# Inverting the diagonal blocks of a chunked delta-rule recurrence 16 wide instead of 32 wide

## The chip, the cores and the metric

The kernel runs on one core of a Trainium2 chip. The core has five instruction streams that matter here: TensorE (PE for its products, PEld for the loading of their stationary operand), VectorE (DVE), ScalarE (ACT), GpSimd (POOL), and SyncE (SP), which issues the DMAs. Each runs its own instructions in the order in which they stand and waits for the others through semaphores. TensorE writes to PSUM only, and VectorE and ScalarE move results from there to SBUF. The metric is the device time of one execution in microseconds (us).

## The reference

An attention-like recurrence over 768 time steps (4 batches, 8 heads, head size 40) makes `y`, which then passes through a gated feed-forward block:

```python
for t in range(S):
    y[:, :, t] = np.einsum('bhd,bhde->bhe', rt, state)
    Sa = np.einsum('bhde,bhe->bhd', state, at)
    state_decay = state * wt[:, :, None, :] - np.einsum('bhd,bhe->bhde', Sa, bt)
    state = state_decay + np.einsum('bhd,bhe->bhde', vt, kt)
...
h = np.maximum(x @ w_in, 0.0)
u, v = (h[..., :d_ff // 2], h[..., d_ff // 2:])
v_n = (v - mu) / np.sqrt(var + 1e-06)
v_s = np.einsum('ts,bsd->btd', w_spatial, v_n) + b_spatial[None, :, None]
gated = u * v_s
return (gated @ w_out).astype(np.float32)
```

Everything is float32. What the state loses at a time step depends on the state that the step before left, so within a chunk of 64 time steps the corrections form a unit lower triangular system of 64 unknowns. Its inverse is what this change is about.

## The kernel before, in words

Phase 1 runs the recurrence and the first half of the feed-forward block, phase 2 the spatial product and the projection. Phase 1 has 24 steps (`NS`): 2 pairs of batches times 12 chunks of 64 times. A step handles 8 units (`NU`), each with two heads, one in the upper and one in the lower 64 partitions (`PR`).

For each step there is preparation and a chain. Preparation, some steps ahead: `prep_load` brings 774 KB of input in two DMAs, `scan1`, `scan2`, `at_mul` and `sl_mul` make `at` and `sl` on VectorE, `lprime` makes the two 32x32 diagonal blocks of each head's 64x64 matrix on TensorE, and `lblock` (L338) masks them on VectorE into `Lc`, which collects four steps (`GS`), a group. Six groups make the 24 steps.

`invert(g)` inverts the 32x32 blocks of a whole group on VectorE: a transpose (L346), thirty pairs of a product (L352, into PSUM as `itmp`) and an addition (L356), and two closing transposes (L361, L363) that give `XT0` and `X11`, the inverse and its transpose. Group 0 is inverted in one go ahead of step 0; the pieces of the later groups are spread over the steps before they are needed.

One step ahead of its use, the two 32x32 inverses of a head are joined into the inverse of its 64x64 matrix: `b_l21` (L459) makes the off-diagonal block, `b_zt` (L478) multiplies it with `XT0`, `b_x21` (L505) multiplies that with `X11`, and `b_xcopy` (three ACT copies, L770) puts the diagonal blocks into `xf`. Around them stand `b_lka` (L390), `b_tok` (L442, two transposes named tok0 and tok1 here) and `b_h` (L420), each with its copies on ACT.

The chain of a step: `c_bp` (L536) multiplies the state `Mc`, ACT copies (L546), `c_ff` (L554), a copy to `ffs` (L562), `c_xx` (L572) with `xf`, the xx copies (L583), POOL's triangular masks (`strict`, L397), `c_mp` (L606, L612), the new `Mc` on VectorE (L626, L630), `c_y` (L638) and its scaling on VectorE (L651). The next step's `c_bp` needs the new `Mc`, and needs L651 to have emptied its PSUM buffer.

The order is written out by hand: `at(t, fn, ...)` gives each piece a place in step time, the list is sorted by it, and each engine receives its instructions in that order. From step 11 on the products of the feed-forward block (L708, L753) are put in at four places of a step. PSUM has eight banks: two for `bk`, which all of `lprime`, `b_lka`, `b_tok`, `b_l21`, `b_zt`, `b_h` and `b_x21` share in turn, two for `ch`, two for `bp`, one each for `itmp` and `pv`. Whoever writes a third `bk` waits until the first has been emptied.

Of the kernel before, what the change touches and what calls it, by code (L numbers as in the profile page):

```python
# [25 lines left out]
GS = 4  # L26
WSEG = C + 2
# [184 lines left out]
def phase1(ctx, tc, early, late, vtok, win, xs, vns, uts, dscr):  # L212
# [14 lines left out]
    inv = pool("inv")  # L227
    xinv = pool("xinv")
# [24 lines left out]
    maskp = const.tile([P, C], F32, name="maskp")  # L253
    maskn = const.tile([P, C], F32, name="maskn")
# [78 lines left out]
    def lblock(s):  # L333
        if s % GS == 0:
            st["Lc", s // GS] = inv.tile([P, GS * NU, HB], F32, name="Lc")
        Lc = st["Lc", s // GS]
        u0 = (s % GS) * NU
        nc.vector.tensor_tensor(  # L338
            out=Lc[:, u0:u0 + NU, :], in0=st.pop(("pl", s)),
            in1=maskl.unsqueeze(1).broadcast_to([P, NU, HB]), op=ALU.mult,  # L340
        )
# [24 lines left out]
    INV_N = HB + 1  # L366
# [35 lines left out]
    def b_lka_out(s, par):  # L402
# [3 lines left out]
        if s in LKA_POOL:  # L406
            nc.scalar.activation(At[par][ev], pk[ev], AF.Copy)  # L407
# [63 lines left out]
    def b_zt(s):  # L471
        XT0, X11 = st["X", s // GS]
        u0 = (s % GS) * NU
        l21 = st["l21", s]
        m2 = ps_k.tile([P, NU, HB], F32, name="bk")
        for n in range(NU):
            for o in (0, 64):
                nc.tensor.matmul(  # L478
                    m2[o:o + HB, n, :], lhsT=l21[o + HB:o + 64, n, :],
                    rhs=XT0[o + HB:o + 64, u0 + n, :], start=True, stop=True,  # L480
# [96 lines left out]
    def c_xx_out(s, g):  # L577
# [3 lines left out]
        if s in TRI_POOL:  # L581
            for par in range(2):
                nc.scalar.activation(Rt[par][PR[par], gp], xx[PR[1 - par]], AF.Copy, scale=-1.0)  # L583
            for par in range(2):
                strict(Rt[par][PR[par], gp, 0:C], NP)
            return
        for par in range(2):
            nc.scalar.activation(Rt[par][PR[par], gp, C:], xx[PR[1 - par], :, C:], AF.Copy, scale=-1.0)
        for par in range(2):
            ur, ev = PR[par], PR[1 - par]  # L590
            nc.vector.tensor_tensor(
                out=Rt[par][ur, gp, 0:C], in0=xx[ev, :, 0:C],
                in1=maskn[ev].unsqueeze(1).broadcast_to([64, NP, C]), op=ALU.mult,
            )
# [178 lines left out]
    H_POOL, LKA_POOL, TRI_POOL = range(0, 99), range(0, 99), range(0, 99)  # L773
# [18 lines left out]
    for q in range(1, NS):  # L792
# [77 lines left out]
    with tc.manual_schedule():  # L870
# [20 lines left out]
        for m, val in ((maskp, 1.0), (maskn, -1.0)):  # L891
            p.memset(m, val)
            for rows in PR:
                p.affine_select(
                    out=m[rows], in_=m[rows], pattern=[[1, C]], base=0,
                    channel_multiplier=-1, compare_op=ALU.is_gt, fill=0.0,
                )
# [111 lines left out]
```

## Time and profile before

| | |
|---|---|
| three runs | 708.47, 710.8 and 714.62 us; median 710.8 |
| span of the profiled execution, first to last instruction | 709.5 us |
| TensorE products and loads | 11,136 each, products busy for 593.6 us (84%) |
| VectorE, ScalarE, GpSimd busy | 437.5, 414.7 and 290.3 us |
| first inversion on VectorE | 28.6 to 56.6 us |
| step ends (end of the second L651) | step 0: 71.3, 3: 145.9, 7: 227.9, 11: 307.1, 15: 388.6, 23: 545.3 us |
| granted TensorE clock, mean | 0.900 |

The execution's own time is not told apart from its span; the span lies among the three runs' times, 1.3 us under their median. A row of a timeline reads: start, length, engine, line, operation, output <- inputs, shape, how many were merged, and in brackets the idle time before it with what ended it. "issue" there is time in which the engine waited for nothing that the profile shows. In the table of busy time by stretch, the clock is the share of full speed that was granted.

### The profile page before, as it was taken

To read this page: it belongs to the slowest core of one execution; us is meant where nothing else is said; L and a number is where in the kernel's file an instruction comes from. 1 tells how busy PE (TensorE), PEld (TensorE's weight loads), DVE (VectorE), ACT (ScalarE), POOL (GpSimd) and SP (SyncE) were. 2 spreads that over 40 slices of the span, in tenths; PEclk is the share of its full clock that TensorE was granted. 3 is DMA by queue.
4 is the path that set the end of the run, shared out by engine and by line. 5 is a ranking of instruction groups with operands and counts; after the bars stand their busy time and mean duration, and the time that the engine had idled before them with its cause. 6 is when DMAs were issued, how large, how long until landed. Compare 5 with 4: busy or idle time off the path is not lost. (4 is left out here: it accounts for less than half of the span.)

```text
span 709.5 us, 26133 instructions
## 1 busy us (share of the span) xinstructions
PE 593.6 (84%) x11136; PEld 538.4 (76%) x11136; DVE 437.5 (62%) x862; ACT 414.7 (58%) x904; POOL 290.3 (41%) x486
## 2 busy tenths in 40 slices
PE   1707886587877789898997999999999999999997
PEld 1606785476766678787886788778888988999997
DVE  7897659977999899766688456612127521332221
ACT  2406754375565777587886889889855543331112
POOL 4102213212345444253464524545457982453221
PEclk9656978787797877899999899999999999999999
DMA  8443665273554724456536434344336454650001
GB/s 188 84 97 56 122 144 103 63 154 73 121 113 93 141 66 115 96 125 127 122 109 209 119 118 121 94 125 138 99 103 186 144 170 129 203 176 29 29 29 55
DMA packets 101339, 81.38 MB, mean 115 GB/s; under 512 B 33576, under 2 KB 90152, under 8 KB 99304
## 3 DMA queue, kind: packets, MB, share of 16 engines
q1 hardware_dynamic: 100680, 78.01, 44.0%
q10 hardware_dynamic: 544, 1.72, 1.1%
q8 instruction: 87, 1.43, 0.9%
q14 instruction: 28, 0.23, 0.1%
HBM read 59.20 MB, written 20.50 MB: 112 GB/s over the span
## 5 line engine op out<-in xcount | busy, mean ns | idle before, releaser
L397 POOL TENSOR_SCALAR_AFFINE_SELECT Rt<-Rt 64x512 f32<-64x512 f32 (+1 forms) x144 | 84.0, 585 | 99.4 <-ACT Rt L583 76.3
L546 ACT ACTIVATE Rt<-bp 64x416 f32<-64x416 f32 x96 | 49.1, 512 | 71.5 <-PE bp L536 69.5
L352 DVE TENSOR_TENSOR itmp<-A 128x30 f32<-128x30 f32 (+9 forms) x180 | 75.3, 419 | 3.2
L397 POOL TENSOR_SCALAR_AFFINE_SELECT At<-At 64x512 f32<-64x512 f32 x48 | 36.3, 756 | 96.5 <-ACT At L407 94.3
L536 PE MATMUL bp<-lin,Mc 40*64 40x104 f32 x768 | 53.5, 302 | 15.4 <-DVE y L651 11.7
L173 PE MATMUL pg<-wsh,vh 128*128 128x384 f32 x192 | 64.7, 337 | 0.0
L174 PE MATMUL pg<-wsl,vh 128*128 128x384 f32 x192 | 64.7, 337 | 0.0
L175 PE MATMUL pg<-wsh,vl 128*128 128x384 f32 x192 | 64.6, 336 | 0.0
L356 DVE TENSOR_TENSOR A<-A,itmp 128x30 f32<-128x30 f32 (+9 forms) x180 | 59.0, 328 | 6.2
L536 PEld LDWEIGHTS bp<-lin,Mc 40*64 40x64 f32 x768 | 46.7, 168 | 18.3 <-DVE y L651 13.7
L177 DVE TENSOR_TENSOR g<-pg,bb 128x384 f32<-128x384 f32 x32 | 17.8, 556 | 62.9 <-PE pg L175 59.1
L54 POOL TENSOR_TENSOR gl<-g,gh 128x384 fp32r<-128x384 f32 x32 | 33.9, 1064 | 50.2 <-ACT gh L50 50.0
L583 ACT ACTIVATE Rt<-ch 64x416 f32<-64x416 f32 x96 | 49.2, 512 | 4.5 <-PE ch L572 2.1
L554 PE MATMUL ch<-Rt,At 128*64 128x104 f32 x768 | 47.5, 283 | 0.0
L554 PEld LDWEIGHTS ch<-Rt,At 128*64 128x64 f32 x768 | 42.1, 158 | 4.5 <-issue 1.9
L50 ACT ACTIVATE gh<-g 128x384 fp32r<-128x384 f32 x32 | 16.6, 522 | 48.9 <-DVE g L178 48.8
L442 PE MATMUL bk<-ident,sl 128*128 128x128 f32 x192 | 31.1, 293 | 16.3 <-ACT tk L448 6.8
L572 PE MATMUL ch<-ffs,xf 64*64 64x104 f32 x768 | 43.4, 267 | 0.1
L54 POOL TENSOR_TENSOR vl<-raw,vh 128x512 fp32r<-128x512 f32 x24 | 32.3, 1353 | 26.2 <-ACT vh L50 13.9
L716 DVE BATCH_NORM_STATS2 bs<-vr 128x6 f32<-128x512 f32 x24 | 16.6, 691 | 41.6 <-ACT vr L710 41.5
L638 PE MATMUL bp<-Rt,tk 128*40 128x64 f32 x768 | 32.5, 240 | 10.1 <-issue 10.1
L572 PEld LDWEIGHTS ch<-ffs,xf 64*64 64x64 f32 x768 | 38.3, 143 | 1.4 <-ACT Rt L583 0.2
(138 smaller groups left out, 1575.5 us busy)
## 6 DMA issues: line engine op xcount, KB each, us to landing
ein<-in_early SPq DMA_DIRECT2D x40, 387.0 KB
lin<-in_late SPq DMA_DIRECT2D x48, 160.0 KB
uts<-ur SPq DMA_DIRECT2D x48, 128.0 KB
vns<-vr SPq DMA_DIRECT2D x24, 256.0 KB
raw<-vns SPq DMA_DIRECT2D x24, 256.0 KB
ut<-uts SPq DMA_DIRECT2D x24, 256.0 KB
Rt<-in_vtok SPq DMA_DIRECT2D x48, 80.0 KB
xs<-y SPq DMA_DIRECT2D x48, 80.0 KB
```

What stands on the lines that cost most here:

```text
L54: eng.tensor_tensor(out=lo, in0=x, in1=hi.bitcast(F32), op=ALU.subtract)
L173: nc.tensor.matmul(pg, lhsT=vh[:, dc], rhs=w_h, start=(i == 0), stop=False)
L174: nc.tensor.matmul(pg, lhsT=vh[:, dc], rhs=w_l, start=False, stop=False)
L175: nc.tensor.matmul(pg, lhsT=vl[:, dc], rhs=w_h, start=False, stop=(i == NT - 1))
L352: nc.vector.tensor_tensor(out=tp, in0=A[:, k + 1:, k:k + 1].broadcast_to([P, m, k]), in1=A[:, k:k + 1, 0:k].broadcast_to([P, m, k]), op=AL ...
L356: nc.vector.tensor_tensor(out=A[:, k + 1:, 0:k], in0=A[:, k + 1:, 0:k], in1=tp, op=ALU.add)
L397: nc.gpsimd.affine_select(out=t, in_=t, pattern=[[0, k], [1, C]], base=0, channel_multiplier=-1, compare_op=ALU.is_gt, fill=0.0,)
L536: nc.tensor.matmul(bp[PR[par], q, :], lhsT=Mc[RR[par], n, :], rhs=li[RR[par], n, C:], start=(q == 0), stop=False, skip_group_check=True,)
L546: nc.scalar.activation(Rt[par][PR[par], gp, :], st["bp", g][PR[par]], AF.Copy)
L554: nc.tensor.matmul(ff[PR[1 - par], q, :], lhsT=At[par][:, n, :], rhs=Rt[par][:, n, :], start=True, stop=True,)
L572: nc.tensor.matmul(xx[ev, q, :], lhsT=xf[ev, n, :], rhs=ffs[ev, q, :], start=True, stop=True,)
L583: nc.scalar.activation(Rt[par][PR[par], gp], xx[PR[1 - par]], AF.Copy, scale=-1.0)
```

## The change

A 32x32 block is itself split into 16x16 quarters. `invert16` inverts the two diagonal quarters on VectorE: fourteen pairs, each working on both quarters at once, instead of thirty. The last two transposes write 16 columns of each block. The off-diagonal quarter is left to TensorE: `b_w` (128 products for a group) multiplies the off-diagonal quarter with the inverse of the first, ACT copies that into the right half of `XT0` with a per-partition factor that blanks the upper rows, and `b_xt`, for each step, lays the two diagonal quarters out with 8 products against a constant and adds the off-diagonal quarter with 32 products. ACT copies its result to `xf` in place of `b_xcopy`. `b_x11` (16 products for a step) transposes the upper block, and ACT puts it into free rows of `l21`. `b_zt` and `b_x21` then read these copies.

This holds for groups 0 to 3, that is steps 0 to 15; groups 4 and 5 are inverted as before. `Lc` moves to a pool of two buffers, since `b_w` reads it after the next group has begun. The two mask constants go, two others (`lowrow`, `half`) come. The branches that were taken for no step go from `b_lka_out`, `b_h_out` and `c_xx_out`.

What moves, first on TensorE in an ordinary step, the middle of step 5 (`bk` are the shared PSUM buffers, `XT_2201` is `XT0` of group 1). Before:

```order
L442 MATMUL bk<-ident,sl 128x128 x8
L459 MATMUL bk<-sl,at 32x32 x16
L572 MATMUL ch<-ffs,xf_131 64x104 x16
L478 MATMUL bk<-XT_1926,l_2603 32x32 x16
L420 MATMUL bk<-lin_136 64x64 x16
```

After:

```order
L525 MATMUL bk<-ident,sl 128x128 x4
L401 MATMUL bk<-XT_2201,half 32x8x16 x8
L408 MATMUL bk<-XT_2201 16x16 x32
L525 MATMUL bk<-ident,sl 128x128 x4
L542 MATMUL bk<-sl,at 32x32 x16
L657 MATMUL ch<-ffs,xf_134 64x104 x8
L427 MATMUL bk<-ident,xf_133 32x32 x16
L657 MATMUL ch<-ffs,xf_134 64x104 x8
L562 MATMUL bk<-xf_133,l_3164 32x32 x16
L509 MATMUL bk<-lin_139 64x64 x16
```

`b_xt` (L401, L408) now stands between the two halves of `b_tok`, and `b_x11` (L427) between the two halves of `c_xx`. The same place on ACT, before:

```order
L562 ACTIVATE ffs<-ch 128x416 x2
L448 ACTIVATE tk<-bk 128x320 x2
L770 ACTIVATE xf_130<-XT_1926 128x8x32
L770 ACTIVATE xf_130<-XT_1926 32x8x32 x2
L468 ACTIVATE l_2603<-bk 32x256 x2
L583 ACTIVATE Rt_134<-ch 64x416
```

After:

```order
L647 ACTIVATE ffs<-ch 128x416 x2
L531 ACTIVATE tk<-bk 128x320 x2
L845 ACTIVATE xf_133<-bk 128x8x32
L845 ACTIVATE xf_133<-bk 32x8x32 x2
L551 ACTIVATE l_3164<-bk 32x256 x2
L435 ACTIVATE l_3164<-bk 32x256 x2
L667 ACTIVATE Rt_137<-ch 64x416
```

The copies to `xf` (L845) now read PSUM, and two copies (L435) have come in ahead of the xx copies. The third place is the start of the first inversion's use, on TensorE between `c_ff` and `c_xx` of step 0. Before:

```order
L442 MATMUL bk<-ident,sl 128x128 x4
L478 MATMUL bk<-XT_557,l_388 32x32 x16
L442 MATMUL bk<-ident,sl 128x128 x4
L505 MATMUL bk<-zt,X_558 32x32 x16
L459 MATMUL bk<-sl,at 32x32 x16
```

After:

```order
L385 MATMUL bk<-X_521,Lc 32x16 x128
L401 MATMUL bk<-XT_520,half 32x8x16 x8
L408 MATMUL bk<-XT_520 16x16 x32
L562 MATMUL bk<-xf_133,l_399 32x32 x16
L427 MATMUL bk<-ident,xf_133 32x32 x16
L590 MATMUL bk<-zt,l_399 32x32 x16
L525 MATMUL bk<-ident,sl 128x128 x4
L401 MATMUL bk<-XT_520,half 32x8x16 x8
L408 MATMUL bk<-XT_520 16x16 x32
L525 MATMUL bk<-ident,sl 128x128 x4
L542 MATMUL bk<-sl,at 32x32 x16
```

`b_w` (L385) has come in ahead of everything that uses the inverse, and tok0 has moved behind `b_x21`.

The diff, cut to its core:

```diff
+QB = 16
+N16 = 4
...
+    linv = pool("linv", 2)
...
-    maskp = const.tile([P, C], F32, name="maskp")
-    maskn = const.tile([P, C], F32, name="maskn")
+    lowrow = const.tile([P, 1], F32, name="lowrow")
+    half = const.tile([P, 2, HB], F32, name="half")
...
-            st["Lc", s // GS] = inv.tile([P, GS * NU, HB], F32, name="Lc")
+            st["Lc", s // GS] = linv.tile([P, GS * NU, HB], F32, name="Lc")
...
+    def invert16(g):
+        Lc = st["Lc", g]
+        A = inv.tile([P, 2 * QB * (HB + 1)], F32, name="A")
+        nc.vector.transpose(
+            out=A[:, 0:HB * HB].rearrange("p (t s) -> p t s", s=HB), in_=Lc.rearrange("p u t -> p t u")
+        )
+        yield
+        nc.vector.memset(A[:, 0:HB * HB:HB + 1], 1.0)
+        D = A.rearrange("p (b x) -> p b x", b=2)[:, :, 0:QB * HB].rearrange("p b (t s) -> p b t s", s=HB)
+        for k in range(1, QB - 1):
+            m = QB - 1 - k
+            tp = ps_i.tile([P, 2, m, k], F32, name="itmp")
+            nc.vector.tensor_tensor(
+                out=tp, in0=D[:, :, k + 1:QB, k:k + 1].broadcast_to([P, 2, m, k]),
+                in1=D[:, :, k:k + 1, 0:k].broadcast_to([P, 2, m, k]), op=ALU.mult,
+            )
+            nc.vector.tensor_tensor(
+                out=D[:, :, k + 1:QB, 0:k], in0=D[:, :, k + 1:QB, 0:k], in1=tp, op=ALU.add
+            )
+            yield
...
+    def b_w(g):
+        Lc = st.pop(("Lc", g))
+        XT0, X11 = st["X", g]
+        mw = ps_k.tile([P, GS * NU, QB], F32, name="bk")
+        for u in range(GS * NU):
+            for o in range(0, P, HB):
+                nc.tensor.matmul(
+                    mw[o:o + HB, u, :], lhsT=Lc[o:o + QB, u, :], rhs=X11[o:o + QB, u, 0:QB],
+                    start=True, stop=True,
+                )
+        st["mw", g] = mw
+
+    def b_w_out(g):
+        nc.scalar.activation(st["X", g][0][:, :, QB:], st["mw", g], AF.Copy, scale=lowrow)
+
+    def b_xt(s):
+        XT0, X11 = st["X", s // GS]
+        u0 = (s % GS) * NU
+        mx = ps_k.tile([P, NU, HB], F32, name="bk")
+        for o in range(0, P, HB):
+            rows = slice(o, o + HB)
+            for blk in range(2):
+                nc.tensor.matmul(
+                    mx[rows, :, blk * QB:(blk + 1) * QB], lhsT=half[rows, blk],
+                    rhs=XT0[rows, u0:u0 + NU, 0:QB], start=True, stop=not blk, skip_group_check=True,
+                )
+        for n in range(NU):
+            for o in range(0, P, HB):
+                rows = slice(o, o + HB)
+                nc.tensor.matmul(
+                    mx[o:o + QB, n, QB:], lhsT=XT0[rows, u0 + n, QB:], rhs=XT0[rows, u0 + n, 0:QB],
+                    start=False, stop=True, skip_group_check=True,
+                )
+        st["mx", s] = mx
+
+    def b_xt_out(s, eng):
+        xf, mx = xfs[s % 2], st["mx", s]
+        eng(out=xf[:, :, HB:], in_=mx)
+        for o in (0, 64):
+            eng(out=xf[o:o + HB, :, 0:HB], in_=mx[o:o + HB])
+        st["XT2", s] = xf[:, :, HB:]
+
+    def b_x11(s):
+        xf = xfs[s % 2]
+        mt = ps_k.tile([P, NU, HB], F32, name="bk")
+        for n in range(NU):
+            for o in (0, 64):
+                rows = slice(o, o + HB)
+                nc.tensor.matmul(
+                    mt[rows, n, :], lhsT=xf[rows, n, 0:HB], rhs=ident[rows, rows], start=True, stop=True,
+                )
+        st["mt", s] = mt
+
+    def b_x11_out(s):
+        st["X21", s] = st["l21", s]
+        for o in (0, 64):
+            nc.scalar.activation(st["l21", s][o:o + HB], st["mt", s][o:o + HB], AF.Copy)
...
+        if q // GS < N16:
+            if z:
+                at(b + 0.76, b_w, q // GS)
+                at(b + 0.78, b_w_out, q // GS)
+            at(b + (0.82 if z else 0.40), b_xt, q)
+            at(b + (0.84 if z else 0.50), b_xt_out, q, XC)
+            at(b + (0.87 if z else 0.56), b_x11, q)
+            at(b + (0.89 if z else 0.58), b_x11_out, q)
+        else:
+            at(b + (0.975 if z else 0.50), b_xcopy, q, XC)
...
-        gen = invert(g)
-        for k in range(INV_N):
-            at(t0 + (t1 - t0) * k / (INV_N - 1), step, gen)
+        gen = invert16(g) if g < N16 else invert(g)
+        for k in range(INV_N[g]):
+            at(t0 + (t1 - t0) * k / (INV_N[g] - 1), step, gen)
...
-        for _ in invert(0):
+        for _ in invert16(0):
...
+        for k, (fn, *args) in enumerate((
+            (b_w, 0), (b_w_out, 0), (b_xt, 0), (b_xt_out, 0, act_copy), (b_zt, 0), (b_x11, 0),
+            (b_zt_out, 0), (b_x11_out, 0), (b_x21, 0), (b_x21_out, 0),
+        )):
+            at(0.392 + 0.0005 * k, fn, *args)
```

More of the change, by code (lines that the diff above doesn't have):

```diff
@@ L341, in lblock @@
         )
+    def invert16(g):
[18 more added lines that the diff above has]
+            yield
+        XT0 = xinv.tile([P, GS * NU, HB], F32, name="XT0")
+        X11 = xinv.tile([P, GS * NU, HB], F32, name="X11")
+        st["X", g] = (XT0, X11)
+        Dd = D[:, :, :, 0:QB]
+        nc.vector.transpose(
+            out=X11[:, :, 0:QB].rearrange("p u s -> p s u"), in_=Dd.rearrange("p b t s -> p s b t")
+        )
+        yield
+        nc.vector.transpose(
+            out=XT0[:, :, 0:QB].rearrange("p u t -> p t u"), in_=Dd.rearrange("p b t s -> p t b s")
+        )
+        yield
@@ L364, in invert @@
         yield
-    INV_N = HB + 1
+    INV_N = [QB + 1 if g < N16 else HB + 1 for g in range(NS // GS)]
     def lin_load(s):
@@ L479, in b_zt @@
                     m2[o:o + HB, n, :], lhsT=l21[o + HB:o + 64, n, :],
-                    rhs=XT0[o + HB:o + 64, u0 + n, :], start=True, stop=True,
+                    rhs=xt[o + HB:o + 64, n, :], start=True, stop=True,
                 )
@@ L500, in b_x21 @@
         u0 = (s % GS) * NU
+        x11 = X11[:, u0:u0 + NU] if s // GS >= N16 else st["X21", s]
         zt = st["zt", s]
@@ L580, in c_xx_out @@
         xx = st["xx", g]
[L581 to L586, printed above, removed]
         for par in range(2):
-            nc.scalar.activation(Rt[par][PR[par], gp, C:], xx[PR[1 - par], :, C:], AF.Copy, scale=-1.0)
+            nc.scalar.activation(Rt[par][PR[par], gp], xx[PR[1 - par]], AF.Copy, scale=-1.0)
         for par in range(2):
[L590 to L594, printed above, removed]
+            strict(Rt[par][PR[par], gp, 0:C], NP)
     def c_mp(s, g):
@@ L890, in phase1 @@
         make_identity(nc, ident)
[L891 to L897, printed above, removed]
         for t in (Mc, *xfs):
             p.memset(t, 0.0)
+        p.memset(lowrow, 1.0)
+        p.memset(half, 0.0)
+        for q in range(P // HB):
+            rows = slice(q * HB, (q + 1) * HB)
+            p.affine_select(
+                out=lowrow[rows], in_=lowrow[rows], pattern=[[0, 1]], base=-QB,
+                channel_multiplier=1, compare_op=ALU.is_ge, fill=0.0,
+            )
+            for blk in range(2):
+                cols = slice(blk * QB, (blk + 1) * QB)
+                nc.scalar.activation(
+                    half[rows, blk, cols], ident[rows, q * HB + blk * QB:q * HB + (blk + 1) * QB], AF.Copy,
+                )
         for q in range(2):
```

37 lines of the change are left out of this document (11 added, 26 removed).

## The prediction

> **What bounds the kernel now.** I read the busy time by stretch first, one stretch for each step (from the end of one step's last y product on VectorE to the next), because the page's averages mix a first phase of many tiny products with a second one of wide ones. Columns: length, then busy time and instructions of PE, PEld, DVE, ACT and POOL, the granted clock, and the DMA share.
>
> ```profile
> 0.00:28.60 28.60, 9.29 (x338) 8.03 (x340) 22.49 (x31) 7.96 (x17) 10.87 (x28) 0.88 0.70 139
> 28.60:56.60 28.00, 9.08 (x160) 8.49 (x156) 25.86 (x64) 5.45 (x10) 2.73 (x4) 0.56 0.45 93
> ...
> 93.10:117.40 24.30, 18.55 (x544) 17.05 (x536) 20.05 (x42) 12.77 (x29) 5.80 (x8) 0.78 0.70 142
> 117.40:145.90 28.50, 16.45 (x452) 14.70 (x450) 27.27 (x57) 12.26 (x27) 5.18 (x8) 0.74 0.37 72
> 145.90:167.50 21.60, 18.41 (x519) 16.95 (x518) 12.81 (x27) 13.31 (x29) 4.27 (x8) 0.74 0.74 158
> ...
> 187.80:208.60 20.80, 16.11 (x465) 14.40 (x456) 19.91 (x39) 13.06 (x29) 8.86 (x10) 0.89 0.58 122
> ...
> 328.70:348.10 19.40, 18.03 (x420) 15.49 (x415) 14.70 (x33) 15.99 (x36) 10.41 (x23) 1.00 0.40 96
> ```
>
> The rows are the loads and scans at the start, the first inversion, and steps 2, 3, 4, 6 and 13. VectorE is the bound in three of them: the first inversion (25.86 of 28.00) and steps 2 and 3 (27.27 of 28.50 in step 3). In step 6 it is just as full (19.91 of 20.80), yet step 4, in which it has 7 us less to do, is no shorter (21.60). So in the middle steps a full VectorE is not what sets the length. From step 12 on TensorE is (18.03 of 19.40).
>
> Next the order in time. This is the first inversion, on VectorE, and the two products that wait for it, directly and at the end:
>
> ```profile
> 28.59 1.95 DVE L346 STREAM_TRANSPOSE A<-Lc 128x1024 f32<-128x1024 f32 x1
> 30.62 0.20 DVE L352 TENSOR_TENSOR itmp<-A 128x30 f32<-128x30 f32 x1
> ...
> 50.92 0.28 DVE L352 TENSOR_TENSOR itmp<-A 128x108 f32<-128x108 f32 x1
> 51.53 0.25 DVE L352 TENSOR_TENSOR itmp<-A 128x84 f32<-128x84 f32 x1
> 52.10 0.23 DVE L352 TENSOR_TENSOR itmp<-A 128x58 f32<-128x58 f32 x1
> 52.61 0.20 DVE L352 TENSOR_TENSOR itmp<-A 128x30 f32<-128x30 f32 x1
> ...
> 53.06 1.91 DVE L361 STREAM_TRANSPOSE XT<-A 128x1024 f32<-128x1024 f32 x1
> 54.83 1.97 DVE L363 STREAM_TRANSPOSE X<-A 128x1024 f32<-128x1024 f32 x1
> ...
> 55.12 1.06 PE L478 MATMUL bk<-XT,l 32*32 32x32 f32 x32 [18.50 <-DVE XT L361]
> 62.59 3.04 PE L572 MATMUL ch<-ffs,xf 64*64 64x104 f32 x32
> ```
>
> And these are the stops of TensorE in steps 2, 3, 6 and 7 that end with VectorE's work; the one on tk goes back to ACT, which waited for a scan on VectorE:
>
> ```profile
> 116.36 2.52 PE L536 MATMUL bp<-lin,Mc 40*64 40x104 f32 x26 [5.75 <-DVE y L651]
> 127.31 0.94 PE L442 MATMUL bk<-ident,sl 128*128 128x128 f32 x4 [3.63 <-ACT tk L448]
> 133.12 1.06 PE L459 MATMUL bk<-sl,at 64*32 64x32 f32 x32 [4.87 <-DVE Lc L338]
> 145.62 2.52 PE L536 MATMUL bp<-lin,Mc 40*64 40x104 f32 x26 [1.55 <-DVE y L651]
> ...
> 207.32 0.66 PE L536 MATMUL bp<-lin,Mc 40*64 40x104 f32 x9 [2.29 <-DVE y L651]
> 223.54 1.06 PE L478 MATMUL bk<-XT,l 32*32 32x32 f32 x32 [2.02 <-DVE XT L361]
> 125.90 0.21 ACT L300 ACTIVATE sc<-S 128x8 f32<-128x8 f32 x1 [2.92 <-DVE S L282]
> ```
>
> The other stops of steps 4 to 10 are of another kind: about once in a step TensorE stops in the middle of a group of products, for nothing that the profile shows (the second row: four such stops at y's products, 10.1 us together).
>
> ```profile
> q8 instruction: 87, 1.43, 0.9%
> ...
> PE bp L638 <- issue: 10.1, 4, 3.2
> ...
> 202.42:207.98 5.56, 2.93 (x129) 2.49 (x127) 5.42 (x15) 1.22 (x3) 1.55 (x2) 1.00 0.70 92
> 207.98:220.42 12.44, 10.94 (x254) 9.85 (x254) 12.13 (x22) 10.41 (x22) 6.80 (x7) 0.86 0.35 98
> ...
> 237.50:245.50 8.00, 5.91 (x211) 5.35 (x210) 7.83 (x19) 5.86 (x14) 5.61 (x9) 1.00 0.98 185
> 245.50:252.50 7.00, 5.85 (x145) 5.53 (x146) 5.18 (x13) 2.11 (x5) 0.00 (x0) 0.61 0.11 26
> ...
> 246.65 0.61 PE L638 MATMUL bp<-Rt,tk 128*40 128x64 f32 x13 [3.24 <-issue]
> ```
>
> The third and fourth rows are stretches from one such stop to the next: 129 and 254 products and as many loads, 256 and 512 instructions. The instruction queue (first row) moved 87 packets, and the page counts 11,136 products and as many loads on TensorE: 256 for each packet. So TensorE had run out of code. The stop at 246.65 comes at the end of 8 us in which the DMA engines were 98% busy (a step's input is being loaded), and after it the clock falls to 0.61. I read it as a fetch that stood behind the load.
>
> **The change, part by part.** *Inversion on VectorE.* The first transpose stays (1.95). Thirty pairs from 30.62 to 53.06 (22.4) become 14 of 28 to 112 elements. Pairs start 0.51, 0.57 and 0.61 us apart at 58, 84 and 108 elements, so 14 take some 7.9. The two closing transposes have half the elements: 1.0 each, if time goes with elements (1.9 if it does not). A group costs 12 instead of 28, four groups save some 64 us on VectorE. That is no gain in itself; only the stops above are.
>
> *Head.* X11 is ready at 28.6 + 2.0 + 7.9 + 1.0 = 39.5. What TensorE then has to do is new, and its price comes from these rows:
>
> ```profile
> 109.86 0.76 PE L327 MATMUL bk<-at,sl 64*32 64x32 f32 x64
> 259.08 0.69 PE L478 MATMUL bk<-XT,l 32*32 32x32 f32 x32
> 257.50 1.64 PE L572 MATMUL ch<-ffs,xf 64*64 64x104 f32 x32
> L487 ACT ACTIVATE zt<-bk 32x256 f32<-32x256 f32 x48 | 17.9, 373 | 8.5 <-PE bk L478 7.8
> ```
>
> A float32 product leaves two records, so L327 is 32 products in 0.76. b_w has 128 of that kind: 3.0, and 4.3 at the half clock of the head. b_xt has 8 products of 128 columns, priced as half of L572's 16 of 104 columns (1.0), and 32 small ones (0.76): 1.8. b_x11 has 16 like L478: 0.7. In the head at half clock: b_w to 44, a fetch stop of some 2 inside (512 instructions without a pause), ACT's copy 0.6, b_xt 3.5, its first copy 0.4, so b_zt at about 50 instead of 55.1. Step 0 then has its own b_xt and b_x11 ahead of the xx product of 62.59. I take 5 us gained (2 to 8).
>
> *Weighed against a rule.* L327's 64 records start in 0.76 us, 12 ns a record. The Trainium skill (TensorE: Matmul & The Clock Gate, "Wait — 56ns, not 53.3ns?") says that matmuls never start less than about 25 ns apart, however few columns they have; by it the 2,816 added records would take 70 us against 34 at 12 ns, and the sum would come to some 745. The trace differs from it here, by half, so it gets no chance of its own.
>
> *Steps 2 and 3.* The five stops sum to 5.75 + 3.63 + 4.87 + 1.55 = 15.8. With 16 us off VectorE in that stretch they go, but ACT's chain is next: I take 13 (8 to 16). *Steps 6 and 7*: 2.29 + 2.02, and the closing transposes stand ahead of Mc: 5 (2 to 6).
>
> *The cost in nine ordinary early steps* (0 to 2, 4 to 6, 8 to 10). The PSUM pool bk has two buffers, and b_xt goes in between the two tok products. Step 9, before:
>
> ```profile
> 255.65 0.66 PE L442 MATMUL bk<-ident,sl 128*128 128x128 f32 x4 [0.42 <-ACT At L407]
> 256.88 0.69 PE L459 MATMUL bk<-sl,at 64*32 64x32 f32 x32 [0.57 <-ACT tk L448]
> 256.40 0.75 ACT L448 ACTIVATE tk<-bk 128x320 f32<-128x320 f32 x2
> 259.00 2.12 ACT L583 ACTIVATE Rt<-ch 64x416 f32<-64x416 f32 x4
> ```
>
> Now b_xt takes the buffer for which the second tok waited (255.65) and ends at 257.4; the second tok follows (0.66), its copy (0.37), then b_xt_out's three copies in place of b_xcopy's and l21_out's two (together 1.85, from the end of tk at 257.15 to 259.00) and the new b_x11_out (two of 0.37). ACT comes to the xx copies at 261.2 instead of 259.0: 2.2 us later, and POOL's masks, the y products and the next step hang on them. But the load's burst does not move. TensorE comes later to where it ran dry, and the stop (2.5 in the mean of those four) gets shorter by as much as it comes later. I take 0.5 a step (-1.8 to 2.2): 4.5.
>
> *Steps 12 to 14.* No stop is left there to absorb it; TensorE is busy for 18.03 of 19.40, so 2.5 of products less some 0.8 of its idle time: 1.7 each (1.1 to 2.5), 5 in all.
>
> *Steps 3, 7 and 11*, where a group begins: 3.0 + 1.8 + 0.7 of products with two turns through ACT, 6.5 in sequence. Part falls in TensorE's idle time (12 us in step 3, length less busy time): 4 each (2 to 8), 12.
>
> *At no cost*: the buffer for Lc; the constants, a dozen short instructions on POOL and ACT at the start (busy 10.87 and 7.96 of 28.60, under VectorE's 22.49; without that cover they would cost 2); the branches dropped in lka_out, h_out and xx_out (never run).
>
> Sum: -5 - 13 - 5 + 4.5 + 5 + 12 = -1.5 us. The profiled span is 709.5 and the median of the three runs 710.8, 1.3 above it: 709.3, say 709.
>
> **The rivals.** *Faster: the stops vanish, and with them the slow clock.* If TensorE comes to the dry place after the burst, a step saves the stop (2.5) and the slow stretch behind it: from 245.5 to 252.5 TensorE is busy for 5.85 us at a clock of 0.61, which is 3.6 at full clock, 2.2 less. The same product at half clock (2.52 at 145.62) and at full:
>
> ```profile
> 328.32 1.38 PE L536 MATMUL bp<-lin,Mc 40*64 40x104 f32 x26
> ```
>
> 2.5 + 2.2 - 2.2 = 2.5 gained a step where I had 0.5 lost; over the six steps from 4 to 10 that is 18: 691. For it: the stop is tied to the burst, and VectorE no longer holds TensorE. Against it: 5,632 more instructions, 22 blocks, have to be fetched. The Trainium skill (TensorE: Matmul & The Clock Gate, "Why this matters for your kernels") says that an idle gap of about 3 us drops the clock to half; the trace agrees, 3.24 idle and then 0.61.
>
> *Slower: nothing is absorbed.* If the denser code runs dry as long as before, since blocks empty faster, each of nine early steps pays 2.2 instead of 0.5: +15, 724. It decides from about 1.5 us a step upward, where the sum passes 718. For it: one stop a step now, and b_w alone empties two blocks. Against it: the burst's end is fixed.
>
> *No change because VectorE was never the bound*: in the middle steps this is already my reading; for steps 2 and 3 the stops name VectorE, so it is no case of its own.
>
> **How the numbers follow.** The forecast has 0.45 (700 to 718), faster 0.27, slower 0.28. About 1% (704 to 718) is what a measurement of this kernel can tell from no change. Of the forecast's 0.45, 0.11 lies under 704 and 0.34 within 1%. Together: faster 0.38, same 0.34, slower 0.28. The range is 688 to 728: past the rivals' own times by 3 to 4 us, so that about a third of each, under 2 in 10 in all, lies outside.
>
> **What would show it.** Right: the inversion pairs end near 38.5 in the head, b_zt starts near 50; the stops of steps 2 and 3 on y, Lc and tk are gone; step 3 ends some 15 us earlier than at 145.9; from there on that lead shrinks. Step 9's xx copies come about 2 us later after the At copies than now. Wrong: steps 4 to 10 under 19 us (the faster rival) or over 22 (the slower), more than one stop for code in a step, or closing transposes of 1.9 each.

## The result, and the profile after

| | before | changed |
|---|---|---|
| runs, us | 708.47, 710.8, 711.03, 714.62 | 751.94, 761.36, 767.9, 768.87 |
| median, us | 710.9 | 764.6 |
| span of the profiled execution, us | 709.5 | 750.2 |

The kernel became slower: the ratio is 1.065, 95% interval 1.054 to 1.076. Two of the four runs of the changed kernel (767.9 and 768.87, mean clock 0.866 and 0.877) are over 1.5% above the fastest; ratios here and below leave such runs out, medians hold all runs. Run again later (d1 below) it took 752.7 beside 703.9 of the kernel before. The forecast was 709 with a range of 688 to 728.

These are the page's lines of busy time and of the instruction queue, and its row of granted clock in 40 slices (tenths of full speed), of the changed kernel:

```profile
PE 644.9 (86%) x13952; PEld 582.2 (78%) x13952; DVE 373.8 (50%) x734; ACT 430.3 (57%) x948; POOL 285.1 (38%) x486
...
PEclk9957776759997778899899989999999999999999
...
q8 instruction: 109, 1.79, 1.1%
```

VectorE has 63.7 us less to do (437.5 before), as was worked out. TensorE has 51.3 more (593.6 before) and 22 more blocks of code (87 before). Next the head, with VectorE's end of the first inversion, and TensorE and ACT behind it:

```profile
39.42 0.18 DVE L362 TENSOR_TENSOR A<-A,itmp 128x28 f32<-128x28 f32 x1
39.64 1.09 DVE L370 STREAM_TRANSPOSE X<-A 128x512 f32<-128x512 f32 x1
40.61 1.00 DVE L374 STREAM_TRANSPOSE XT<-A 128x512 f32<-128x512 f32 x1
...
40.88 2.21 PE L385 MATMUL bk<-X,Lc 16*32 16x16 f32 x149 [4.23 <-DVE X L370]
47.58 1.62 PE L385 MATMUL bk<-X,Lc 16*32 16x16 f32 x106 [4.49 <-issue]
...
54.42 0.69 PE L408 MATMUL bk<-XT 32*16 32x16 f32 x60 [4.10 <-issue]
55.60 0.91 PE L562 MATMUL bk<-xf,l 32*32 32x32 f32 x26 [0.49 <-ACT xf L845]
...
49.34 0.69 ACT L392 ACTIVATE XT<-bk,lowrow 128x512 f32<-128x512 f32 x1 [5.62 <-PE bk L385]
55.16 1.02 ACT L845 ACTIVATE xf<-bk 128x256 f32<-128x256 f32 x3 [5.13 <-PE bk L408]
```

What TensorE waits for is there 14 us earlier than before: X at 40.7, where it was XT at 55.0. Then `b_w` (L385) stops in its middle for 4.49 us and `b_xt` (L408) for 4.10, both for nothing that the profile shows, and `b_zt` starts at 55.60, where it had started at 55.12. ACT waits behind each of the two. So 8.6 of the 14 us went into two stops for code, and the rest into the new products and copies.

The stretches of steps 2, 3, 4, 6 and 13, as the prediction showed them of before (columns as there):

```profile
99.90:125.60 25.70, 21.85 (x640) 19.45 (x630) 15.54 (x29) 13.51 (x31) 4.26 (x8) 0.71 0.67 124
125.60:154.80 29.20, 21.66 (x824) 19.62 (x814) 17.73 (x36) 13.68 (x30) 6.79 (x8) 0.78 0.50 94
154.80:179.20 24.40, 21.40 (x681) 19.24 (x672) 12.39 (x24) 13.82 (x31) 5.00 (x8) 0.77 0.59 123
198.40:217.60 19.20, 16.45 (x532) 14.38 (x528) 14.95 (x28) 13.69 (x31) 8.54 (x10) 0.91 0.55 128
366.40:388.30 21.90, 20.87 (x567) 18.01 (x559) 14.86 (x34) 16.71 (x38) 9.88 (x23) 0.98 0.40 93
```

VectorE bounds none of them any more (17.73 of 29.20 in step 3, where it was 27.27 of 28.50), but only step 6 is shorter (19.20 instead of 20.80), and the four others are longer: TensorE is now the fullest engine, at a clock of 0.71 to 0.78 in the first three. The view of waits names TensorE's stops by line and cause (sum, times, longest); of the changed kernel first, and one row of before:

```profile
PE bk L385 <- issue: 15.1, 6, 4.5
...
PE bk L408 <- issue: 5.6, 2, 4.1
...
PE bk L485 <- issue: 4.7, 5, 2.0
PE bk L590 <- issue: 4.2, 2, 2.7
PE bk L385 <- DVE X L370: 4.2, 1, 4.2
...
PE bp L621 <- DVE y L726: 0.8, 1, 0.8
```

```profile
PE bp L536 <- DVE y L651: 11.7, 4, 5.8
```

The wait for y is down from 11.7 us to 0.8. The stops for code (rows that end with issue) have moved into the new products and grown. That these rows are stops for code can be read from the traces, which also hold the times of the instruction queue's packets: each of the 29 stops of the changed kernel ends 1.2 to 1.7 us after such a packet has landed, and so does each of the 16 before.

Summed by cause over all of TensorE's gaps above 0.1 us in the trace, and with the products' busy time beside them, TensorE's time is accounted for almost fully. The same sums of the experiments that follow stand with them (us, one profiled execution each). What is missing to the span, 5.0 to 5.7 us, is mostly the 4.1 to 4.4 behind the last product, then stops on POOL and DMA and shorter gaps. The last column is the mean granted clock:

| profiled execution | products | waits on VectorE | on ACT | stops for code | span | clock |
|---|---|---|---|---|---|---|
| before | 593.6 | 55.7 | 29.7 | 25.4 | 709.5 | 0.900 |
| changed | 644.9 | 23.9 | 30.2 | 46.3 | 750.2 | 0.902 |
| d1, changed, executed again | 645.4 | 23.7 | 27.6 | 38.9 | 741.0 | 0.902 |
| a2, two groups | 612.8 | 31.2 | 28.1 | 41.8 | 719.2 | 0.918 |
| a3, few wide products | 611.6 | 25.2 | 34.4 | 26.3 | 702.7 | 0.940 |
| a4, before and extra products | 616.7 | 46.9 | 23.5 | 40.3 | 733.8 | 0.899 |
| b1, before without loads | 577.2 | 67.7 | 30.2 | 3.7 | 683.9 | 0.937 |
| b2, changed without loads | 629.0 | 27.5 | 29.1 | 20.7 | 711.3 | 0.925 |
| b3, before with split loads | 580.5 | 63.4 | 33.7 | 5.2 | 689.0 | 0.931 |
| b4, changed with split loads | 619.8 | 25.6 | 29.3 | 27.2 | 707.0 | 0.946 |
| c1, few wide products, split loads | 606.5 | 31.0 | 38.3 | 4.3 | 685.5 | 0.950 |
| c3, group 1 alone, split loads | 593.1 | 49.8 | 33.6 | 12.5 | 694.8 | 0.921 |
| c4, before, loads in eight | 581.7 | 80.7 | 36.8 | 3.8 | 708.4 | 0.929 |
| d2, spread over the step | 658.3 | 27.2 | 34.4 | 42.5 | 767.4 | 0.884 |
| d3, spread, split loads | 638.2 | 28.9 | 33.8 | 17.2 | 723.7 | 0.909 |

From the first row to the second: 51.3 more in products, 31.8 less in waits on VectorE, 0.5 more on ACT, 20.9 more for code, together 40.9 of the 40.7 by which the span grew. The saving on VectorE came; products and code took more than it. How much code took differs between two executions of the same kernel: 20.9 more here, 13.5 more in d1.

Part of a difference in products is the clock. Multiplied by the mean clock, the products come to 580 to 586 us in the six rows with the changed arithmetic (changed, d1, b2, b4, d2, d3) and to 534 to 541 in the four with the arithmetic before. So an estimate from these rows is some 45 us of new products at full clock (rough, for the mean is over the whole span).

### The profile page after: what moved, and what is told of

The parts are those of the page before. It is cut to its first block, busy times and chain, and to the rows that moved or that the text cites. A ratio compares the mean times of both kernels' runs of the same rounds, so it can differ in the third digit from the quotient of the medians.

```text
span 750.2 us, 31701 instructions
## 1 busy us (share of the span) xinstructions
PE 644.9 (86%) x13952; PEld 582.2 (78%) x13952; DVE 373.8 (50%) x734; ACT 430.3 (57%) x948; POOL 285.1 (38%) x486
## 3 DMA queue, kind: packets, MB, share of 16 engines
q8 instruction: 109, 1.79, 1.1%
## 5 line engine op out<-in xcount | busy, mean ns | idle before, releaser
L492 POOL TENSOR_SCALAR_AFFINE_SELECT Rt<-Rt 64x512 f32<-64x512 f32 (+1 forms) x144 | 81.6, 568 | 137.5 <-ACT Rt L667 102.8
L492 POOL TENSOR_SCALAR_AFFINE_SELECT At<-At 64x512 f32<-64x512 f32 x48 | 33.5, 697 | 97.3 <-ACT At L501 95.2
L56 POOL TENSOR_TENSOR gl<-g,gh 128x384 fp32r<-128x384 f32 x32 | 33.4, 1050 | 47.0 <-ACT gh L52 46.9
L657 PE MATMUL ch<-ffs,xf 64*64 64x104 f32 x768 | 49.1, 278 | 1.0 <-issue 1.0
L701 DVE TENSOR_TENSOR Mc<-ch,scn 104x160 f32<-104x160 f32 x22 | 9.6, 436 | 80.0 <-PE ch L687 27.4
L726 DVE TENSOR_TENSOR y<-bp,Et 104x256 f32<-104x256 f32 x48 | 20.1, 422 | 58.2 <-PE bp L713 57.9
L621 PE MATMUL bp<-lin,Mc 40*64 40x104 f32 x768 | 45.9, 275 | 2.8 <-issue 1.6
L639 PE MATMUL ch<-Rt,At 128*64 128x104 f32 x768 | 44.1, 267 | 0.0
L621 PEld LDWEIGHTS bp<-lin,Mc 40*64 40x64 f32 x768 | 40.1, 149 | 4.7 <-DVE y L726 2.1
L639 PEld LDWEIGHTS ch<-Rt,At 128*64 128x64 f32 x768 | 38.4, 145 | 4.3 <-issue 1.7
L56 POOL TENSOR_TENSOR vl<-raw,vh 128x512 fp32r<-128x512 f32 x24 | 31.9, 1340 | 22.9 <-ACT vh L52 20.9
L330 PE MATMUL bk<-at,sl 64*32 64x32 f32 x1536 | 22.4, 215 | 18.2 <-DVE sl L317 14.4
```

The lines of the kernel that those rows point to most:

```text
L56: eng.tensor_tensor(out=lo, in0=x, in1=hi.bitcast(F32), op=ALU.subtract)
L492: nc.gpsimd.affine_select(out=t, in_=t, pattern=[[0, k], [1, C]], base=0, channel_multiplier=-1, compare_op=ALU.is_gt, fill=0.0,)
L621: nc.tensor.matmul(bp[PR[par], q, :], lhsT=Mc[RR[par], n, :], rhs=li[RR[par], n, C:], start=(q == 0), stop=False, skip_group_check=True,)
L639: nc.tensor.matmul(ff[PR[1 - par], q, :], lhsT=At[par][:, n, :], rhs=Rt[par][:, n, :], start=True, stop=True,)
L657: nc.tensor.matmul(xx[ev, q, :], lhsT=xf[ev, n, :], rhs=ffs[ev, q, :], start=True, stop=True,)
```

## Experiments

Two theories stood at the start. *Code*: TensorE uses up its code faster with the many small products, and stops until the next block is there. *Turns*: the new products and copies lengthen the chain between TensorE and ACT through the two bk buffers. The kernel before ran beside each set of runs, at 703.9 to 707.6 us in the median; ratios are to it.

### a1 and a2: which groups

```diff
-N16 = 4
+N16 = 0
...
-        for _ in invert16(0):
+        for _ in invert(0):
```

> All six groups are inverted 32 wide again; the new pool for Lc, the two new constants and the places in the plan stay as in the changed kernel. Both theories (code: the 5,632 new instructions on TensorE use up its code faster, and it stops for the next block; turns: the new products and copies make a longer chain of TensorE and ACT through the two bk buffers) put the whole loss on the 16 wide groups, so both expect the time of the kernel before, 711 within 1%. If the rest of the change costs something, 718 or more.

Measured: 705.8 us beside 707.6, ratio 1.009 (0.999 to 1.019). The buffer, the constants and the plan's other edits cost nothing that these runs can tell; the interval leaves room for 2%.

```diff
-N16 = 4
+N16 = 2
```

> Only groups 0 and 1 are inverted 16 wide. By the lags of the traces the changed kernel is 9 us behind at the end of step 6, before the products of group 2 begin, and 40.7 at the end. Both theories expect some 9 to 15 us over the kernel before, 720 to 726. If the loss comes from the later groups alone, 711 or less.

Measured: 717.4, ratio 1.024 (1.000 to 1.049), a little under what was expected. By the medians the loss grows with the number of groups. By the table, groups 0 and 1 bring 24.5 of the 31.8 us saved in waits on VectorE; groups 2 and 3 add 32 us of products and save 7.3.

### a3: few wide products in the same places

```diff
-        for u in range(GS * NU):
-            for o in range(0, P, HB):
-                nc.tensor.matmul(
-                    mw[o:o + HB, u, :], lhsT=Lc[o:o + QB, u, :], rhs=X11[o:o + QB, u, 0:QB],
+        for o in range(0, P, HB):
+            nc.tensor.matmul(
+                mw[o:o + HB], lhsT=Lc[o:o + QB, 0, :], rhs=X11[o:o + QB, :, 0:QB],
...
-                    mx[o:o + QB, n, QB:], lhsT=XT0[rows, u0 + n, QB:], rhs=XT0[rows, u0 + n, 0:QB],
+                mx[o:o + QB, :, QB:], lhsT=XT0[rows, u0, QB:], rhs=XT0[rows, u0:u0 + NU, 0:QB],
...
-                    mt[rows, n, :], lhsT=xf[rows, n, 0:HB], rhs=ident[rows, rows], start=True, stop=True,
+                mt[rows], lhsT=ident[rows, rows], rhs=xf[rows, :, 0:HB], start=True, stop=True,
```

> The changed kernel, in which the many small products are replaced by a few wide ones that write the same parts of the same PSUM buffers: 4 in place of 128 for the off-diagonal quarter of a group, 4 in place of 32 for each step's quarter, 2 in place of 16 for the transposed upper block. Every copy, buffer and wait stays; the inverses are no longer the right ones. Code theory: the stops that came with the change go and the stops of VectorE stay gone, 690 to 712. Turns theory: the chain is as long as before, 740 or more.

Measured: 703.6 us, ratio 1.002 (0.992 to 1.012). With every turn through ACT still there, the loss is gone; the turns theory falls as the main cause. This profile also shows what the prediction had expected of VectorE. Steps 2 and 3:

```profile
87.00:106.00 19.00, 16.16 (x564) 13.66 (x549) 15.70 (x30) 13.41 (x31) 5.41 (x8) 1.00 0.80 160
106.00:127.90 21.90, 17.50 (x505) 14.38 (x494) 17.54 (x36) 13.63 (x30) 6.66 (x8) 0.84 0.67 125
```

Together 40.9 us instead of 52.8 (24.30 and 28.50), and step 3 ends at 127.9 instead of 145.9. The lead of 18 us shrinks to 7 by the end of the program: even the wide products are 35.9 us of TensorE's time in the groups by line (5.1, 11.6, 7.2 and 12.0).

### a4: extra products in the kernel before

These are 872 of the change's 1,408 products, by number and size.

```diff
+    def dummy(parts):
+        pv = ps_m.tile([P, DH], F32, name="pv")
+        for n, k, m in parts:
+            for j in range(n):
+                o = (j % 4) * HB
+                nc.tensor.matmul(
+                    pv[o:o + m, 0:k], lhsT=ident[o:o + HB, o:o + m], rhs=ident[o:o + HB, 0:k],
+                    start=True, stop=True,
+                )
...
+        if q < 12:
+            if z:
+                at(b + 0.76, dummy, [(128, 16, 32)])
+            at(b + (0.82 if z else 0.40), dummy, [(8, 128, 32), (32, 16, 16)])
+            at(b + (0.87 if z else 0.56), dummy, [(16, 32, 32)])
```

> The kernel before, with as many extra products put in at the places of the new ones (128 at the start of a group, 56 in every step, for steps 1 to 11), which read a constant and write a PSUM bank that nobody reads there; no copy, no wait and no use of bk comes with them. Code theory: the changed kernel's lag at the end of step 10 (29 us, with 15 of VectorE's stops saved) comes back without that saving, 740 or more. Turns theory: the products alone cost their own time, some 2 us a step less what falls into idle time, 715 to 730.

Measured: 736.9 us, ratio 1.056 (1.040 to 1.072), just under the code theory's figure and clearly over that of turns. Products that nobody waits for, with no copy and no buffer shared, cost 29 us by themselves. Their group by line:

```profile
L764 PE MATMUL pv<-ident 32*16 32x16 f32 (+3 forms) x1744 | 27.6, 204 | 11.5 <-issue 11.4
```

27.6 us of products and 11.4 of stops for code inside them; in the whole execution these stops went from 25.4 to 40.3, and the waits on VectorE and on ACT fell by 8.8 and 6.2, which is what was absorbed.

### b1 to b4: the loads

```diff
-        if q + 2 < NS:
-            at(t + 0.50, prep_load, q + 2, 48)
...
-        prep_load(4, 48)
-        prep_load(5, 48)
```

> The kernel before without the input loads of steps 4 to 23: the steps compute on the input of steps 0 and 1, which stays in the two buffers. If TensorE's stops for code come from a fetch that stands behind a load, most of the 25 us of them go, and the slow clock behind them: 680 to 698. If its code is simply used up faster than it can be fetched at any time, they stay: 705 to 712.

> The changed kernel without the same loads. If the added stops for code (46 us of them in all, 21 more than before) come from fetches behind loads: under 20 us of stops are left, and the time is 705 to 725, some 20 to 30 over the kernel before without loads, which is the time of the added products themselves. If dense code empties the buffer by itself: 40 us of stops or more are left, and the changed kernel stays 45 or more over the kernel before without loads.

Measured: the kernel before without loads 687.9 us, ratio 0.977 (0.971 to 0.983); the changed one 707.3, ratio 1.003 (0.998 to 1.007). The table has the stops: 25.4 to 3.7 us in the one, 46.3 to 20.7 in the other. So nearly all of the stops before, and about half of those after (46.3, and 38.9 in d1), hang on the loads. The two kernels are now 19.3 us apart instead of 48.8 (752.7 and 703.9). But 20.7 us of stops stay where no load is left: dense small products also run their code dry by themselves.

```diff
-            at(t + 0.50, prep_load, q + 2, 48)
+            for k in range(4):
+                at(t + 0.30 + 0.15 * k, prep_load, q + 2, 48, slice(k * EW // 4, (k + 1) * EW // 4))
```

> The kernel before with each step's load in four pieces of 194 KB, 0.15 of a step apart, in place of one of 774 KB. If the stops are fetches behind a load, a fetch now stands behind a quarter of it: stops half as long, 695 to 706. If not: 711 within 1%.

> The changed kernel with its loads in the same four pieces. If the stops are fetches behind a load: 735 to 750, and less of them than the 46 us of the changed kernel. If not: 752 to 768 as in the changed kernel.

Measured: the kernel before with split loads 690.6 us, ratio 0.981 (0.976 to 0.985), better than forecast and the fastest that leaves nothing out; the changed one 718.0, ratio 1.021 (1.014 to 1.028), also better. The second half of the first `b_w` shows the three cases, here b4 and then b2, against 4.49 in the changed kernel:

```profile
45.69 1.62 PE L385 MATMUL bk<-X,Lc 16*32 16x16 f32 x106 [2.67 <-issue]
```

```profile
44.91 1.62 PE L385 MATMUL bk<-X,Lc 16*32 16x16 f32 x106 [1.57 <-issue]
48.74 0.68 PE L408 MATMUL bk<-XT 32*16 32x16 f32 x60 [1.09 <-issue]
49.92 0.91 PE L562 MATMUL bk<-xf,l 32*32 32x32 f32 x26 [0.49 <-ACT xf L845]
```

In b2 `b_zt` starts at 49.92, the forecast's 50, with two stops of 1.57 and 1.09 where it had put one of some 2. What the pieces help by (shorter queues, smaller packets or the pauses between) was not told apart. In the kernel before, part of what the stops took goes to VectorE: the waits on it went from 55.7 to 63.4.

### c1 and c2: what VectorE's saving is worth, and which products cost

c1 is a3 with the loads of b4.

> The changed kernel with the few wide products of a3 (the same parts of the inverses are wrong) and with its loads in four pieces: VectorE's work is gone, nearly no products have come, and fetches stand behind short loads only. If VectorE's saving is worth what the stops of TensorE on it say once the code does not hide it (63 us of such stops in b3, 27 in b2): 660 to 678. If the chain through ACT takes it back: 685 or more, no better than the kernel before with split loads (691).

Measured: 683.1 us, ratio 0.966 (0.960 to 0.972), between the two figures. Against b3 the waits on VectorE are 32.4 us less, the products 26.0 more and the waits on ACT 4.6 more. So even with few products and short loads the saving is nearly eaten by TensorE's own time; 7.5 us are left (medians of two sets of runs, beside 705.8 and 707.1 of the kernel before).

```diff
-        for u in range(GS * NU):
-            for o in range(0, P, HB):
-                nc.tensor.matmul(
-                    mw[o:o + HB, u, :], lhsT=Lc[o:o + QB, u, :], rhs=X11[o:o + QB, u, 0:QB],
+        for o in range(0, P, HB):
+            nc.tensor.matmul(
+                mw[o:o + HB], lhsT=Lc[o:o + QB, 0, :], rhs=X11[o:o + QB, :, 0:QB],
```

> The changed kernel, loads as they were, in which the 128 products of the off-diagonal quarter, once in a group, are 4 wide ones; the products of every step stay. It leaves out the right value of that quarter. 992 of the 2,336 records that a3 left out are gone. If every added record costs the same: 20 to 24 us under the changed kernel, 730 to 742. If the loss is the bursts of 512 instructions: 715 to 725. If it is the products of the steps and their turns: 745 or more.

Measured: 723.3 us, ratio 1.012 (1.001 to 1.023), where the burst of 512 instructions had its figure. `b_w` has 42% of the records that a3 leaves out (992 of 2,336), yet without them the loss falls from 6.5% (d1) to 1.2%.

### c3 and c4: versions that might beat both

c3 has the loads of b4 and 16 wide inversion in group 1 alone.

```diff
-N16 = 4
+G16 = (1,)
...
-        if q // GS < N16:
+        if q // GS in G16:
```

> A version that might beat both: group 1 alone is inverted 16 wide (its inversion is what fills VectorE in steps 2 and 3), the other five 32 wide, and the loads come in four pieces. b3, all 32 wide with split loads, took 691. If the stops on VectorE of steps 2 and 3 (some 16 us) outweigh one burst of 128 products and four steps of 56: 680 to 689. If the products cost what they did in the changed kernel, some 11 us a group with their stops: 690 to 698.

Measured: 694.5 us, ratio 0.982 (0.975 to 0.988), no better than b3. Even the one group whose inversion fills VectorE does not pay: against b3 the waits on VectorE are 13.6 us less, the products 12.6 and the stops for code 7.3 more.

c4 is the kernel before with eight pieces, 0.08 of a step apart from 0.305 on.

> The kernel before with each step's load in eight pieces, 0.08 of a step apart. If the stop is the time that a fetch stands behind one piece: 683 to 690, near the kernel before with no loads (688). If four pieces had removed all there is, or if the issues on SP cost more: 690 or more.

Measured: 707.0, ratio 1.001 (0.997 to 1.005): no gain. Its stops for code are gone as in b3 (3.8 us), but the last pieces come too late, and VectorE waits for them; from its view of waits:

```profile
DVE sl L314 <- DMA ein<-in_early: 18.0, 4, 6.2
```

### d1 to d3: burst or number

d1 is the changed kernel again. d2 makes `b_w`'s 128 products in four lots of 32, one for each step of a group; each has its own copy on ACT, so 12 copies come in. d3 is d2 with the loads of b4.

```diff
-            if z:
-                at(b + 0.76, b_w, q // GS)
-                at(b + 0.78, b_w_out, q // GS)
+            tw = q - q % GS + (-0.24, 0.20 if q > GS else 0.398, 0.60, 0.92)[q % GS]
+            at(tw, b_w, q)
+            at(tw + 0.001, b_w_out, q)
```

> The changed kernel as it is, so that it stands beside the next two in one row of runs. Both theories: 6.5% over the kernel before, 745 to 765.

> The changed kernel, in which the 128 products for the off-diagonal quarters of a group come in four lots of 32, one for each step of the group, at four places of a step, each with a copy of its own on ACT. Nothing is left out, as many products as before. If the burst of 512 instructions is what empties TensorE's code: 720 to 738, near the 723 of c2. If the number of instructions counts: 745 or more.

> The same with the loads in four pieces. If the burst and the long loads together are the whole loss: 688 to 705, against 718 of b4. If the number of instructions counts: 715 to 722, no better than b4.

Measured: d1 752.7 us, ratio 1.065 (1.055 to 1.076); d2 771.5, ratio 1.094 (1.085 to 1.104); d3 731.6, ratio 1.043 (1.033 to 1.053). The burst theory falls: the same products without the burst cost more, not less, and 42.5 us of stops for code are left, where the changed kernel had 46.3 and d1 38.9. d3 lies above both of its figures: against b4 its stops are 10.0 us less, but its products 18.4 more. The stops move elsewhere; from d2's view of waits:

```profile
PE bk L330 <- issue: 14.6, 6, 5.3
...
PE bk L566 <- issue: 5.0, 2, 4.4
...
PE bk L386 <- ACT xf L603: 4.7, 3, 2.4
...
PE bk L386 <- issue: 3.6, 2, 2.0
```

L330 is `lprime`, 64 records that were in the kernel all along; L566 is `b_zt`, and `b_w` (L386) itself has only 3.6 of them. So the stop falls on whoever stands where a block ends. The 4.7 us on ACT are new turns for the bk buffers, so d2 does not hold the number of turns fixed. Its products are those of d1 and take 12.9 us longer, at a clock of 0.884 instead of 0.902 (times the clock, both come to 582); why the clock was lower is not shown. Why `b_w` costs more than its share of the records in c2 stays open.

## Why the prediction was wrong, point by point

*VectorE, right.* The pairs end at 39.6 (38.5 was worked out), the closing transposes take 1.09 and 1.00 (1.0), VectorE's work falls by 63.7 (64). The waits that end with VectorE fall by 31.8 us. 14.3 of it is the head's (18.5 to 4.2), where X at 39.5 instead of XT at 55.0 made 15.5; the other 17.5 stand against the 18 of steps 2, 3, 6 and 7. (The stops behind these steps that the prediction sums to 15.8 are four, not five.)

*The prices of the products, right.* The prediction's prices come to 52 us in all (four times 3.0, sixteen times 1.8 + 0.7). The groups by line of the changed kernel:

```profile
L427 PE MATMUL bk<-ident,xf 32*32 32x32 f32 x512 | 14.8, 215 | 2.4 <-issue 2.0 <-ACT xf L845 0.2
L401 PE MATMUL bk<-XT,half 32*32 32x128 f32 x256 | 13.4, 318 | 7.5 <-ACT At L501 5.7 <-issue 1.8
L408 PE MATMUL bk<-XT 32*16 32x16 f32 x1024 | 13.0, 180 | 5.6 <-issue 5.6
L385 PE MATMUL bk<-X,Lc 16*32 16x16 f32 x1024 | 12.8, 193 | 19.3 <-issue 15.1 <-DVE X L370 4.2
```

14.8 + 13.4 + 13.0 + 12.8 = 54.0 us. That is 19 ns for each of 2,816 records, where the nearest row gave 12. The rule that the prediction set aside says 25 at least (the Trainium skill, TensorE: Matmul & The Clock Gate, "Wait — 56ns, not 53.3ns?"). Its 745 is near what was measured only by luck: the products take 16 us less than its 70. Besides, the prediction held the 70 against 34 us at 12 ns a record, though its own prices come to 52; against these the rule adds 18, and the sum is 727.

*The step that failed: "the stop gets shorter by as much as it comes later. I take 0.5 a step".* Of 52 us of products the sum took 21.5 in the steps (4.5 + 5 + 12) and laid the rest beside stops and idle time, part of it in the head. The account shows otherwise: TensorE's products took 51.3 us more for 54.0 of new ones, and the stops for code, which were to shrink, grew by 20.9 (by 13.5 in d1). The reasoning had the load's burst as a fixed window that TensorE could come to later. The sum left out what its own rivals named: 5,632 more instructions end 22 more blocks, each of which can meet a load. And a fetch takes time without a load too (b2: 20.7 us of stops). a4 shows both costs without any part of the change: 27.6 us of products, 14.9 more of stops, and 15.0 less of waits on VectorE and ACT.

*The slower rival, right in kind and too small.* "Nothing is absorbed" gave 724 with 2.2 a step. The -5 of the head was already less its new products. With 15.5 in its place and all 52 us on the path, the sum would have been -15.5 - 13 - 5 + 52 = 18.5 and the time 729; with 20.9 of stops it is 750, where the profiled run took 752. The signs that the prediction named for this rival came: steps 4, 8 and 10 were 24.4, 25.8 and 22.8 us long (over 22), though 5, 6 and 9 only 19.1 to 20.6, and step 3 has three stops for code.

*Head: right until the code ran out.* `b_zt` at 55.6 instead of 50. The term "a fetch stop of some 2 inside" was two stops of 4.49 and 4.10. In b2 it starts at 49.92, in a3, which has no stop there, at 45.77:

```profile
45.77 0.91 PE L559 MATMUL bk<-xf,l 32*32 32x32 f32 x26 [0.50 <-ACT xf L842]
```

*Steps 2 and 3: the gain was there and was spent.* In a3 they take 11.9 us less, in the changed kernel 2.1 more (25.70 + 29.20 against 52.8).

*Step 9: 2.2 us later was to be, 4.0 it was.* This is the time from the start of the copy of At to that of the xx copies, on ACT. Here are the copy of At in the kernel before (its xx copies stand in the prediction, at 259.00), then the changed kernel, then a3:

```profile
254.39 1.21 ACT L407 ACTIVATE At<-bk 64x512 f32<-64x512 f32 x2
```

```profile
276.66 1.21 ACT L501 ACTIVATE At<-bk 64x512 f32<-64x512 f32 x2
...
280.30 0.44 ACT L531 ACTIVATE tk<-bk 128x320 f32<-128x320 f32 x1 [1.21 <-PE bk L525]
...
284.47 0.76 ACT L435 ACTIVATE l<-bk 32x256 f32<-32x256 f32 x2 [1.75 <-PE bk L427]
285.26 2.12 ACT L667 ACTIVATE Rt<-ch 64x416 f32<-64x416 f32 x4
...
280.79 1.06 PE L542 MATMUL bk<-sl,at 64*32 64x32 f32 x32 [0.53 <-ACT tk L531]
```

```profile
244.01 1.21 ACT L498 ACTIVATE At<-bk 64x512 f32<-64x512 f32 x2
...
250.62 2.12 ACT L664 ACTIVATE Rt<-ch 64x416 f32<-64x416 f32 x4
```

4.61 us lay between them before (254.39 to 259.00), 8.60 in the changed kernel, 6.61 in a3. The turns that were worked out (2.2) are what a3 shows (2.0). The other 2.0 are TensorE: it works without a pause from 280.79 on, at a granted clock of 0.50 (280.3 to 285.3; before, 0.98 from 253.6 to 259.0). The group L542 takes 1.06 us, its like in step 9 before 0.69, and ACT waits for TensorE at L531 and L435.

*Steps 7 and 11, and 12 to 14.* From one last y product on VectorE to the next, steps 7 and 11 became 8.4 and 4.6 us longer (19.3 to 27.7 and 21.7 to 26.3; 4 each forecast), steps 12 to 14 together 9.3 (59.3 to 68.6; 5 forecast): TensorE was full there, and the products took more than the 1.7 a step that the sum allowed for them.

*The other rival*, stops and slow clock both gone, needed the absorption as well and fell with it. That VectorE was not the bound in the middle steps fits the runs, but no run shows it by itself: with fewer waits on VectorE and hardly a stop, c1 takes as long over steps 4 to 10 as b3 (137.4 us each), and it has more products.

## What to carry to other kernels

Count instructions as well as time when work moves to an engine that is already full: work of the right price can still lie wholly on the path, and each 256 instructions of it want a fetch that can meet a load. Before taking "it hides in a stop" as a term, ask what makes the stop, and whether the new work makes more of them. Where stops without a named cause come beside long loads, see in the trace when the packets of the instruction queue start and land, and try shorter loads first: that edit to the plan gave 1.9% here, where the change to the arithmetic lost 6.5%.

## What the runs showed of the hardware

A stop for code grew and shrank with the load beside it: 4.49 us at the same instruction with a whole load, 2.67 with the load in four pieces, 1.57 with none. So fetches are not always hidden: 25.4 us of one execution before and 46.3 of one changed went into such stops. The Trainium skill (Runtime: NRT & Kernel Launch, "Instruction fetch mechanics") holds that the pace of the instructions covers the fetch; these runs differ. The queue's 109 packets and 1.79 MB are 16.4 KB each. The same section of the Trainium skill gives blocks of 16 KiB, or 256 instructions, and the trace agrees.

What the load delays is the start of the fetch, as the times of the packets show (us; the two stops of the head, with the length of each stop in brackets):

| | changed | b4, split loads | b2, no loads |
|---|---|---|---|
| `b_w` starts | 40.88 | 40.81 | 41.13 |
| packet, start to landing | 44.77 to 46.05 | 42.91 to 44.23 | 42.27 to 43.44 |
| TensorE goes on | 47.58 (4.49) | 45.69 (2.67) | 44.91 (1.57) |
| next packet | 51.68 to 53.05 | 46.98 to 48.20 | 46.01 to 47.29 |
| TensorE goes on | 54.42 (4.10) | 49.80 (1.36) | 48.74 (1.09) |

The second packet starts 4.10 us after TensorE has gone on with a whole load, 1.29 with pieces and 1.10 with none; the packet itself takes 1.2 to 1.4 us in all three. In b2 3.83 us pass from one going on to the next, and the instructions between last 2.74 of them, so a stop is left without any load. In the changed kernel the DMA engines are full up to 50.0 (0.98) and mostly idle from there to the end of the second stop (0.24); its packet starts at 51.68:

```profile
36.00:50.00 14.00, 5.29 (x282) 4.68 (x279) 13.38 (x24) 2.00 (x5) 1.07 (x2) 0.63 0.98 167
...
50.00:54.40 4.40, 0.32 (x8) 0.13 (x5) 0.62 (x1) 0.03 (x1) 0.00 (x0) 0.50 0.24 41
```

Pieces of load can also be too many: eight, spread as far as c4 spread them, removed the same stops and made the data late by as much.
